# Batch transform moved into the first block of each batch, its half sums to the front of VectorE's tiles, two-product values in second blocks

## The chip, the cores and the metric

The kernel runs on one core of a Trainium2 chip. The metric is the device time of one execution in microseconds, median of three runs. The core's engines work in parallel, each through its own stream of instructions in order: TensorE (PE; its weight loads are listed as PEld), VectorE (DVE), ScalarE (ACT), GpSimd (POOL) and SyncE (SP, which here only issues DMAs). Matmul results land in PSUM, eight banks of 128 x 512 float32; GpSimd cannot read them.

## What is computed

```python
def _attn_ref(x):                       # x: (8, 3008, 256)
    X = np.fft.fft(x, axis=1)
    X = np.fft.fft(X, axis=2)
    return X.real.astype(np.float32)

def _moe_ref(x, w_gate, w_val, w_out):  # x: (24064, 256), 256 -> 1536 -> 256
    gate = np.maximum(x @ w_gate, 0.0)
    val = x @ w_val
    return (gate * val @ w_out).astype(np.float32)
```

The real part of a two-dimensional Fourier transform of each of 8 batches goes into a gated feed-forward layer.

## The kernel before, in words

**Mathematics.** The transform along the sequence is folded by symmetry into a cosine part U and a sine part V, 128 channels by 1505 columns each, one column per pair of rows s and S - s. The transform along the channels is folded into the weights: WA (cosine) and WB (sine), index 0 for the gate and 1 for the value; WM is -2 times WB except in its row 0. So for one chunk f of 128 of the 1536 hidden features, WA·U + WB·V is the hidden row of the "plus" half and WA·U - WB·V that of the "minus" half. What belongs to channel 128 is kept in one row per batch, spread over the partitions in a tile CB, and added by a per-partition scale b2.

**Tiles.** In batch 0 the columns go in four segments. From batch 1 on they go in three blocks, `thirds`: 512, 512 and 481 columns. A block has 12 tiles, one for each chunk `fi`. A tile makes both halves of the hidden h for its columns. The call `slot(cur, mid, nxt, after, outs, fold_us)` (L1072) writes the instructions of one tile's time: it finishes `pending` (the tile before), makes the value of `cur`, and prepares the gates of the two after. The order in which a slot issues work is the order on each engine. The parts, by line:

- `sine_part` (L1018): a product into bank g (L1021), copied to SBUF by ScalarE (L1024). `seed` (L1011): ScalarE puts the channel-128 part into a bank p (L1016). `cosine_part` (L1026): one product added to it (L1028).
- `both` (L1030): VectorE makes the gate of the plus half (L1032), GpSimd that of the minus half (L1033).
- `value` (L924): two products into a bank v (L876, L877); VectorE's `relu_mult` (L912) multiplies gate and value into h. One tile later `mirror` adds a third product (L882) so that v holds the minus half's value, and a second `relu_mult` reads it. That is five products of 512 columns for a plain tile: L1021, L1028, L876, L877, L882.
- A **two-product value** (`st["short"]`) uses bank d, of which there is one: ScalarE seeds it (`seed_value`, L1049), one product makes the cosine part (`value_cosine`, L1053), ScalarE copies twice that to SBUF (L1054), a second product completes the plus half (`value_sine`, L1058). The minus half is the difference, taken by VectorE in `value_second`: back into d where `own` is set (L1065), with VectorE's multiplication behind it, or into SBUF (L1067), with GpSimd's multiplication behind it (L1068) and a Relu of the gate on ScalarE (L1129). Such a tile has four products.
- A **"j" tile** makes its gate without g and without `both`: ScalarE copies twice the cosine part out of p (L1039), a second product completes it (L1043), ScalarE copies that (L1044), GpSimd subtracts (L1045). Its products are five.

In batches 2 to 5 the third block (`blk == 2`) is "mixed": tiles 2 and 8 have two-product values with `own`, tiles 5 and 11 are j tiles. The third block of batch 6 and the first two of batch 7 have two-product values in tiles 2, 6 and 10 (`SHORT`), the last block of batch 7 in 2, 5 and 8.

**Output products.** The h of a finished block are multiplied by `wo` during the next block: `todo_out` holds these steps (L784, 256 columns each), 96 for a block or 84 where the last block of a batch leaves one unit less. A slot issues `outs` of them, five eighths between its sine and its cosine product and the rest at its end. ScalarE copies a finished pair out (L797, the queue `evict`, one per slot), and SP sends it to memory.

**The transform of the next batch.** `dft_steps` makes 24 products, eight groups of three (L589), all into bank d: for each of two families, V and then U, a group for one parity, which ScalarE copies to `es` (L598), then a group added to it for the other, which ScalarE casts to the result (L601) and from which VectorE makes the other result in two half sums (L603). `DFT_EVEN[at]` says how many steps are issued behind slot `at` (0 to 35) of a batch: three behind 0, 2, 6, 8, 12, 14, 18 and 20. The copies go to the front of `evict`, the half sums to `sums`, and a slot runs one of each at its end. Two DMAs of the next batch's CB and of row 0 of its V ride on step 21.

**The folds.** GpSimd folds the rows of the batch after next (`fold_steps`): each step has a cost in units, 20.8 in all, and each slot gives `fold_us` of credit, .72, until they are used up. Among the steps SP is told to load the mirrored rows of the batch after that (`load_reversed`, L189, into XG) and to write the reversed copy of a later one (`reverse`, L180, to xr). The first readers of XG are the next batch's `fold_a` (L198).

Of the kernel before, what the change touches and what calls it, by code (L numbers as in the profile page):

```python
# [34 lines left out]
def kernel(  # L35
# [8 lines left out]
    nc = tc.nc  # L44
    B, S, D = x.shape
# [411 lines left out]
    for t in range(3):  # L457
        n = ROWS[1][t]
# [98 lines left out]
            return dst[:, 0:NJ], dst[:, NJ:2 * NJ]  # L557
        return dst[:, 3 * NJ:4 * NJ + 1], dst[:, 2 * NJ:3 * NJ]

    evict, sums = [], []  # L560

    def flush():
        for todo in (evict, sums):
            while todo:
                todo.pop(0)()

# [3 lines left out]
    def family(b, dst, fam, sine, now=True, pool=None):  # L570

        n, cols = (NE, slice(0, NE)) if fam == 0 else (NJ, slice(NE, NK))
        src, tab = (GG[b % 2], tabS) if sine else (FF[b % 2], tabC)
        st, apart = {}, now or pool is not None

        def mm(par, t, nyq=False):
            if par not in st and not apart and not par:
                st[0] = st[1]  # L580
            elif par not in st:
                home, tag = pool or ((psG, "g") if now and not par else (psD, "d"))
                st[par] = home.tile([128, 512], F32, name=tag, tag=tag)
            rows = slice(0, ROWS[par][t])
            if nyq:
                nc.tensor.matmul(st[par][0:1, 0:n], lhsT=FF[b % 2][rows, fam, t, par, 128:129], rhs=tabC[rows, 2 * t + par, cols],
                                 start=False, stop=(t == 2), skip_group_check=True)
            else:
                nc.tensor.matmul(st[par][:, 0:n], lhsT=src[rows, 1 - fam if sine else fam, t, par, 0:128],  # L589
                                 rhs=tab[rows, 2 * t + par, cols], start=(t == 0 and (apart or par == 1)), stop=(t == 2),  # L590
                                 skip_group_check=not apart)
                if b > 2 and (fam, sine, par, t) == (0, False, 0, 2):
                    widen(st[par], n)

        def end(par):
            if par:
                st["es"] = rp.tile([128, NE], F32, name="es", tag="es", bufs=2)
                evict.insert(0, lambda: nc.scalar.copy(st["es"][:, 0:n], st[1][:, 0:n]))  # L598
            elif not apart:
                whole, rest_ = half_of(dst, fam)  # L600
                evict.insert(0, lambda: nc.scalar.copy(whole, st[1][:, 0:n]))  # L601
                for c in (slice(0, NJ // 2), slice(NJ // 2, NJ)):
                    sums.append(lambda c=c: nc.vector.scalar_tensor_tensor(rest_[:, c], in0=st["es"][:, c], scalar=2.0, in1=st[1][:, c],  # L603
                                                                           op0=ALU.mult, op1=ALU.subtract))
            else:
                for d, op in zip(half_of(dst, fam), (ALU.add, ALU.subtract)):
                    m = d.shape[-1]
                    sums.append(lambda d=d, op=op, m=m: nc.vector.tensor_tensor(d, st["es"][:, 0:m], st[0][:, 0:m], op=op))
            if now:
                flush()  # L610

        def at(par):
            home, tag = pool
            st[par] = home.tile([128, 512], F32, name=tag, tag=tag)
            return st[par]
        return mm, end, at

    def dft_first(U, V):

        raw, ends = [], [family(0, dst, 1, False, now=False, pool=pool) for dst, pool in ((U, (psP, "p")), (V, (psO, "o")))]  # L620
        bank = {(k, par): ends[k][2](par) for k in range(2) for par in (1, 0)}

        def products(t, k, rs):
            src, tab = ((FF[1], tabC), (GG[1], tabS))[k]
            for r, par in [(r, par) for r in rs for par in (1, 0)]:
                rows = slice(0, ROWS[par][t])
                nc.tensor.matmul(bank[k, par][:, 0:NJ], lhsT=src[rows, r, t, par, 0:128], rhs=tab[rows, 2 * t + par, odd_k],
                                 start=(t == 0 and r == 0), stop=(t == 2 and r == 1), skip_group_check=bool(k))

        def nyquist(t):  # L630
            for par in (1, 0):
                rows = slice(0, ROWS[par][t])
                nc.tensor.matmul(bank[1, par][0:1, 0:NJ], lhsT=ny[rows, t, par:par + 1], rhs=tabC[rows, 2 * t + par, odd_k],
                                 start=False, stop=False, skip_group_check=True)

        def combine(i, js):
            for j in js:
                home, tag = ((psV, "v"), (psV, "v"), (psG, "g"), (psD, "d"))[len(raw)]
                p = home.tile([128, 512], F32, name=tag, tag=tag)
                for kc in range(2):  # L640
                    nc.tensor.matmul(p[:], lhsT=(TA, TB)[j][:, kc, :], rhs=wr[i][0][:, kc, :], start=(kc == 0), stop=(kc == 1))
                raw.append(p)

        def whole(W, p):
            return W[:, 0:512], p[:]

        products(0, 0, (0,))
        products(0, 1, (0,))
        whole_128(0)
        angle(4, 5)  # L650
        products(0, 0, (1,))
        products(0, 1, (1,))
        nyquist(0)
        angle(5, 4)
        whole_128(1)
        for T in (TA, TB):
            nc.scalar.copy(T[:, 1, 0::2], T[:, 0, 0::2])
            nc.scalar.mul(T[:, 1, 1::2], T[:, 0, 1::2], -1.0)
        products(1, 0, (0, 1))
        products(1, 1, (0, 1))  # L660
        nyquist(1)
        combine(0, (0, 1))
        nc.scalar.copy(*whole(WA[0], raw[0]))
        whole_128(2)
        products(2, 0, (0, 1))
        ends[0][1](1)
        ends[0][1](0)
        evict.pop(0)()
        nc.vector.tensor_scalar(m2[:], pidx[:], scalar1=1.0, op0=ALU.min, scalar2=-2.0, op1=ALU.mult)
        sums[0]()  # L670
        nc.scalar.copy(*whole(WB[0], raw[1]))
        nyquist(2)
        products(2, 1, (0, 1))
        ends[1][1](1)
        ends[1][1](0)
        evict.pop(0)()
        sums[2]()
        combine(1, (0, 1))
        nc.scalar.copy(*whole(WA[1], raw[2]))
        nc.scalar.copy(*whole(WB[1], raw[3]))  # L680
        for k in (1, 3):
            sums[k]()
        del sums[:]
# [160 lines left out]

    DFT_0 = (0, 0, 0, 0, 0, 3, 0, 0, 4, 3, 3, 0), (0, 0, 0, 0, 0) + (1,) * 7, (3, 3, 3, 3, 3, 3, 0, 0, 0, 0, 0, 0)

    DFT_EVEN = (3, 0, 3, 0, 0, 0) * 4 + (0,) * 12
    DFT_1 = (3, 0, 3, 0, 0, 0) * 4 + (0, 1, 0, 1, 1) + (0,) * 7
    todo_out, todo_dft, todo_fold = [], [], []
    credit, paired = 0, False  # L850
    pending = None
# [7 lines left out]
    def run_one(todo):  # L859
        if todo:  # L860
            todo.pop(0)()
# [134 lines left out]
    SHORT = (2, 6, 10)  # L996

    def new_tiles():
        for b in range(1, B):
            for blk, block in enumerate(thirds):  # L1000
                for fi in range(NF):
                    st = tile_of(block, fi, uv[b])
                    st["b"] = b
                    mixed = 1 < b < 6 and blk == 2
                    st["kind"] = "o" if (b, blk, fi) == (1, 0, 6) else "j" if mixed and fi in (5, 11) else "n"
                    st["own"] = mixed
                    st["short"] = mixed and fi in (2, 8) or (b, blk) in ((6, 2), (7, 0), (7, 1)) and fi in SHORT or (b, blk) == (7, 2) and fi in (2, 5, 8)
                    st["lead"] = (b, blk, fi) == (1, 0, 0)
                    yield st

# [61 lines left out]
    def slot(cur, mid, nxt, after, outs, fold_us):  # L1072

        joined, ready = (st is not None and st["kind"] == "j" for st in (nxt, mid))
# [5 lines left out]
            run(todo_out, len(todo_out) - stop + outs * part // 8)  # L1080
        old = nxt is not None and nxt["kind"] == "o"
        new = nxt is not None and nxt["kind"] == "n"
        if old:
            gate(nxt)
        lead = cur["lead"]
# [44 lines left out]
        if nxt is not None and nxt["short"]:  # L1130
            seed_value(nxt)
        run_fold(fold_us)
        if not joined:
            run_one(evict)
        run_one(sums)
        out(8)
        return cur

# [1 line left out]
    tiles, ahead = new_tiles(), []  # L1140

    for b in range(B):
# [4 lines left out]
        for blk, block in enumerate(blocks):  # L1147
            hs = []
            if (b, blk) == (0, 1):
                todo_dft = dft_steps(0, U, V, (0,), nyq=True, now=True)  # L1150
# [69 lines left out]
            else:  # L1220
                for fi in range(NF):
                    at = NF * blk + fi
                    cur = ahead.pop(0)
                    add_h(cur, hs)
                    ahead.append(next(tiles, None))
                    outs = per_tile + ((-2, 0, -2, 2, 2, 0)[fi % 6] if per_tile == 7 else 0)
                    if (b, blk) == (B - 1, 2) and fi > 8:
                        outs = (10, 9, 19)[fi - 9]
                        if fi == 9:
# [5 lines left out]
                        nc.scalar.mul(WV[:, f], WM[1][:, f], -0.5)  # L1235
                    if (b, at) == (2, 0):
                        nc.sync.dma_start(out=WB[0][0:1, :], in_=WM[0][0:1, :])
                    pending = slot(cur, *ahead, outs, .72)
                    for step in more_1.get(at, ()) if b == 1 else ():
                        step()  # L1240
                    run(todo_dft, DFT_1[at] if b == 1 else DFT_EVEN[at])
# [44 lines left out]
```

## Time and profile before

| | |
|---|---|
| median of three runs | 625.36 us (625.28 to 625.39) |
| the profiled execution | 625.38 us |
| its span | 623.5 us |
| instructions | 12412 |
| granted TensorE clock, mean | 1.000 |
| busy VectorE / ScalarE / GpSimd | 547.9 / 473.6 / 516.4 us |

The profile is of one execution. Starts and lengths of instructions are recorded; the ends of matmuls are modelled, so neighbouring matmuls overlap in the record and the time of one is read from start to start. VectorE's and ScalarE's records overlap a little too where one instruction follows on another. A few matmul records can be missing. "Busy" of a window is the time in which the engine has at least one instruction.

### The profile page before, as it was taken

How to read it: one execution, taken by the hardware profiler on the slowest of the kernel's cores; microseconds unless marked ns; L12 is line 12 of the kernel's file. 1: busy time of each engine (PE TensorE's matmuls, PEld its weight loads, DVE VectorE, ACT ScalarE, POOL GpSimd, SP SyncE). 2: the span in 40 equal slices, each digit the busy share in tenths (PEclk: the TensorE clock that was granted, in tenths of full speed). 3: DMA queues.
4: the chain of work that ended last, by engine and by line, in shares of the span. 5: the costliest groups of instructions: out<-in, count | busy, mean ns of one | idle time of the engine just before them, and what ended most of it. 6: DMA issues, size and time to landing. Idle time of an engine off the chain costs nothing.

```text
span 623.5 us, 12412 instructions
## 1 busy us (share of the span) xinstructions
PE 614.8 (99%) x4043; PEld 396.4 (64%) x4087; DVE 547.9 (88%) x978; ACT 473.6 (76%) x878; POOL 516.4 (83%) x490
## 2 busy tenths in 40 slices
PE   8999999999999999999999999999999999999997
PEld 2566666566666666666666666666666666666666
DVE  8886677999899899988999999999999999999991
ACT  7796667777778778776887778777787768999982
POOL 8988992998899988799879989799886656888881
PEclk9999999999999999999999999999999999999999
DMA  9965658744264427315362425211211111211113
GB/s 241 213 200 135 169 181 92 183 88 144 85 152 143 131 71 178 122 45 167 79 189 69 142 77 120 64 54 49 77 44 55 43 61 37 61 52 53 44 51 104
DMA packets 86034, 66.48 MB, mean 107 GB/s; under 512 B 41639, under 2 KB 69063, under 8 KB 85970
## 3 DMA queue, kind: packets, MB, share of 16 engines
q1 hardware_dynamic: 81384, 60.02, 35.4%
q0 software_dynamic: 3984, 4.92, 4.0%
q8 instruction: 32, 0.52, 0.4%
q10 hardware_dynamic: 602, 0.75, 0.4%
q14 instruction: 32, 0.26, 0.1%
HBM read 41.89 MB, written 34.17 MB: 122 GB/s over the span
## 4 chain that ended last, share of the span: by engine, by line
PE 95%; DVE 1%; POOL 1%; issue 1%; DMA 1%; ACT 0%; DVEq 0%; POOLq 0%; ACTq 0%
PE o L784 38%; PE v L882 10%; PE v L877 10%; PE p L1028 8%; PE g L1021 8%; PE v L876 8%; PE d L589 4%; PE p L882 1%; PE p L876 1%; PE p L877 1%; DMA XG<-in_x_dram,gidx 1%; PE d L1053 1%; PE d L1058 1%; PE o L427 1%; POOL XG L120 1%
## 5 line engine op out<-in xcount | busy, mean ns | idle before, releaser
L1033 POOL TENSOR_TENSOR r<-r 128x512 f32<-128x512 f32 (+1 forms) x243 | 302.7, 1253 | 80.2 <-DVE r L1032 77.3
L784 PE MATMUL o<-wo,h 128*128 128x256 bf16 x2172 | 329.6, 273 | 0.2
L912 DVE SCALAR_TENSOR_TENSOR h<-r,v 128x512 bf16<-128x512 f32 (+1 forms) x462 | 294.3, 675 | 38.2 <-PE v L882 32.3
L784 PEld LDWEIGHTS <-h 128*128 128x128 bf16 x2220 | 216.6, 98 | 110.6 <-issue 0.9
L1016 ACT ACTIVATE p<-CB,b 128x512 f32<-128x512 bf16 (+1 forms) x251 | 172.1, 686 | 51.5 <-DVE r L1032 49.6
L1024 ACT COPY r<-g 128x512 f32<-128x512 f32 (+1 forms) x243 | 140.4, 578 | 48.3 <-PE g L1021 41.5
L1032 DVE SCALAR_TENSOR_TENSOR r<-r,p 128x512 f32<-128x512 f32 (+1 forms) x243 | 163.1, 671 | 0.8 <-ACT r L1024 0.8
L877 PE MATMUL v<-V,WB 128*128 128x512 bf16 (+3 forms) x273 | 100.1, 367 | 2.1
L1028 PE MATMUL p<-U,WA 128*128 128x512 bf16 (+1 forms) x251 | 94.1, 375 | 0.0
L1021 PE MATMUL g<-V,WM 128*128 128x512 bf16 (+1 forms) x243 | 91.2, 375 | 0.2
L882 PE MATMUL v<-V,WM 128*128 128x512 bf16 (+1 forms) x232 | 87.0, 375 | 0.2 <-DVE h L912 0.2
L876 PE MATMUL v<-U,WA 128*128 128x512 bf16 (+3 forms) x237 | 86.4, 365 | 0.0
L901 DVE TENSOR_TENSOR h<-r,v 128x376 bf16<-128x376 f32 (+2 forms) x90 | 46.2, 547 | 16.4 <-PE v L882 10.5
L876 PEld LDWEIGHTS <-WA 128*128 128x128 bf16 x328 | 31.9, 97 | 36.1 <-issue 13.4
L797 ACT COPY os<-o 128x512 f32<-128x512 f32 x92 | 52.5, 570 | 2.9 <-issue 2.9
L198 POOL TENSOR_TENSOR XG<-XG,XD 128x510 f32<-128x510 f32 x42 | 52.9, 1268 | 0.8 <-DMA XG<-xr 0.8
L892 ACT ACTIVATE r<-p 128x376 f32<-128x376 f32 (+1 forms) x80 | 38.3, 487 | 18.0 <-PE p L882 8.6
L877 PEld LDWEIGHTS <-WB 128*128 128x128 bf16 x328 | 31.9, 97 | 31.4 <-ACT WB L680 0.2
L206 POOL TENSOR_TENSOR AA<-XG 128x510 f32<-128x510 f32 x42 | 45.3, 1092 | 0.0
L1021 PEld LDWEIGHTS <-WM 128*128 128x128 bf16 x243 | 23.8, 98 | 5.6 <-issue 0.3
L1028 PEld LDWEIGHTS <-WA 128*128 128x128 bf16 x251 | 24.5, 98 | 3.3 <-issue 0.2
L882 PEld LDWEIGHTS <-WM 128*128 128x128 bf16 x233 | 22.8, 98 | 3.6
(201 smaller groups left out, 534.8 us busy)
## 6 DMA issues: line engine op xcount, KB each, us to landing
out_dram<-os SPq DMA_DIRECT2D x124, 128.0 KB
xr<-in_x_dram SPq DMA_DIRECT2D x12, 768.0 KB
XG<-xr SPq DMA_DIRECT2D x12, 768.0 KB
XD<-in_x_dram SPq DMA_DIRECT2D x15, 512.0 KB
out_dram<-os SPq DMA_DIRECT2D x35, 112.0 KB
XD<-in_x_dram SPq DMA_DIRECT2D x8, 448.0 KB
CB<-ch SPq DMA_DIRECT2D x7, 376.2 KB
out_dram<-os SPq DMA_DIRECT2D x13, 96.0 KB
```

Of the source, the lines that this page charges most:

```text
L198: e.tensor_tensor(XG[p, r, t, ::-1, 1:D], XG[p, r, t, ::-1, 1:D], XD[p, r, t, :, D - 1:0:-1], op=ALU.add)
L784: nc.tensor.matmul(st["p"][0:m, q, :], lhsT=lhs(f), rhs=wo[:, f, :], start=(f == 0 and not (early and q)), stop=(f == NF - 1), skip_group_ ...
L876: nc.tensor.matmul(bank[:, 0:st["n"]], lhsT=WA[i][:, st["f"]], rhs=st["us"], start=True, stop=False)
L877: nc.tensor.matmul(bank[:, 0:st["n"]], lhsT=WB[i][:, st["f"]], rhs=st["vs"], start=False, stop=True)
L882: nc.tensor.matmul(bank[:, 0:st["n"]], lhsT=W[i][:, st["f"]], rhs=v, start=False, stop=True, skip_group_check=True)
L912: nc.vector.scalar_tensor_tensor(half_h(st, sign), in0=st["s"][1 + sign][:, 0:n], scalar=0.0, in1=st["v"][:, 0:n], op0=ALU.max, op1=ALU.mult)
L1016: nc.scalar.activation(st["p"][:, 0:st["n"]], st["c"], ACTF.Copy, scale=b2[:, st["fi"]:st["fi"] + 1])
L1021: nc.tensor.matmul(st["g"][:, 0:n], lhsT=WM[0][:, st["f"]], rhs=st["vs"], start=True, stop=True)
L1024: nc.scalar.copy(q[:, 0:n], st["g"][:, 0:n])
L1028: nc.tensor.matmul(st["p"][:, 0:n], lhsT=WA[0][:, st["f"]], rhs=st["us"], start=False, stop=True, skip_group_check=True)
L1032: nc.vector.scalar_tensor_tensor(sp[:, 0:n], in0=q[:, 0:n], scalar=-0.5, in1=st["p"][:, 0:n], op0=ALU.mult, op1=ALU.add)
L1033: nc.gpsimd.tensor_tensor(sm[:, 0:n], sp[:, 0:n], q[:, 0:n], op=ALU.add)
```

## The change

The kernel keeps every operation's form; it changes where they stand and which tiles use which form.

- `DFT_EVEN` becomes three steps behind slots 0, 1, 3, 4, 6, 7, 9 and 10, so that the eight groups stand in the first block of batches 2 to 6. (Batch 1 has a table of its own and stays.)
- The transform's ScalarE copies get a queue of their own, `turned_out`. From batch 2 on a slot starts with one step of it and one half sum (two when no transform step is left); before batch 2 both stay at the end of the slot.
- The second block of batches 2 to 5 becomes mixed like the third, and the second block of batch 6 gets two-product values in tiles 2, 6 and 10.
- From batch 2 on the output products are issued in the pattern -1, -1, +2 around the mean in first blocks (except batch 7's) and evenly elsewhere.
- The credit of the folds becomes .76 a slot in first blocks and .54 in the others, from batch 2 on.

```diff
-    evict, sums = [], []
+    evict, sums, turned_out = [], [], []
...
-        for todo in (evict, sums):
+        for todo in (turned_out, evict, sums):
...
-                evict.insert(0, lambda: nc.scalar.copy(st["es"][:, 0:n], st[1][:, 0:n]))
+                turned_out.append(lambda: nc.scalar.copy(st["es"][:, 0:n], st[1][:, 0:n]))
...
-                evict.insert(0, lambda: nc.scalar.copy(whole, st[1][:, 0:n]))
+                turned_out.append(lambda: nc.scalar.copy(whole, st[1][:, 0:n]))
...
-    DFT_EVEN = (3, 0, 3, 0, 0, 0) * 4 + (0,) * 12
+    DFT_EVEN = (3, 3, 0) * 4 + (0,) * 24
...
-                    mixed = 1 < b < 6 and blk == 2
+                    mixed = 1 < b < 6 and blk > 0
...
-                    st["short"] = mixed and fi in (2, 8) or (b, blk) in ((6, 2), (7, 0), (7, 1)) and fi in SHORT or (b, blk) == (7, 2) and fi in (2, 5, 8)
+                    st["short"] = mixed and fi in (2, 8) or (b, blk) in ((6, 1), (6, 2), (7, 0), (7, 1)) and fi in SHORT or (b, blk) == (7, 2) and fi in (2, 5, 8)
...
         new = nxt is not None and nxt["kind"] == "n"
+        early = cur["b"] > 1
+        if early:
+            run_one(turned_out)
+            run_one(sums)
+            if not todo_dft:
+                run_one(sums)
...
-        if not joined:
+        if turned_out and not early:
+            run_one(turned_out)
+        elif not joined:
             run_one(evict)
-        run_one(sums)
+        if not early:
+            run_one(sums)
...
-                    outs = per_tile + ((-2, 0, -2, 2, 2, 0)[fi % 6] if per_tile == 7 else 0)
+                    if b < 2:
+                        outs = per_tile + ((-2, 0, -2, 2, 2, 0)[fi % 6] if per_tile == 7 else 0)
+                    else:
+                        outs = per_tile + (0 if blk or b == B - 1 else (-1, -1, 2)[fi % 3])
...
-                    pending = slot(cur, *ahead, outs, .72)
+                    pending = slot(cur, *ahead, outs, .72 if b < 2 else (.76, .54, .54)[blk])
```

More of the change, by code (lines that the diff above doesn't have):

```diff
@@ L667, in dft_first @@
         ends[0][1](0)
-        evict.pop(0)()
+        turned_out.pop(0)()
         nc.vector.tensor_scalar(m2[:], pidx[:], scalar1=1.0, op0=ALU.min, scalar2=-2.0, op1=ALU.mult)
@@ L675, in dft_first @@
         ends[1][1](0)
-        evict.pop(0)()
+        turned_out.pop(0)()
         sums[2]()
```

## The prediction

> **What bounds the kernel now.** I read the page first (share of each engine), then the tensor engine's own timeline inside one tile, then the busy time by stretches of one block, and last the waits. The page:
>
> ```profile
> PE 614.8 (99%) x4043; PEld 396.4 (64%) x4087; DVE 547.9 (88%) x978; ACT 473.6 (76%) x878; POOL 516.4 (83%) x490
> ```
>
> The ends of matmuls are modelled, so the 99% proves little alone. The timeline of TensorE through one tile of batch 2 (start, length, what) settles it:
>
> ```profile
> 206.05 0.71 PE L784 MATMUL o<-wo,h 128*128 128x256 bf16 x5
> 206.60 0.38 PE L1028 MATMUL p<-U,WA 128*128 128x512 bf16 x1
> 206.81 0.38 PE L882 MATMUL v<-V,WM 128*128 128x512 bf16 x1
> 207.03 0.38 PE L876 MATMUL v<-U,WA 128*128 128x512 bf16 x1
> 207.25 0.38 PE L877 MATMUL v<-V,WB 128*128 128x512 bf16 x1
> 207.46 0.49 PE L784 MATMUL o<-wo,h 128*128 128x256 bf16 x3
> 207.79 0.65 PE L589 MATMUL d<-tabS,G 128*128 128x377 bf16 x3
> 208.27 0.38 PE L1021 MATMUL g<-V,WM 128*128 128x512 bf16 x1
> 208.49 0.71 PE L784 MATMUL o<-wo,h 128*128 128x256 bf16 x5
> ```
>
> Starts, not lengths, give the price. From 206.60 to 207.46 four products of 512 columns start 0.215 us apart; five output products take 206.60 - 206.05 = 0.55, so 0.109 each; three transform products take 208.27 - 207.79 = 0.48, so 0.160 each. Nothing stands between them: TensorE streams, and a plain 512-column tile lasts 8 x 0.109 + 5 x 0.215 = 1.95 us. So this kernel's time in these batches is a count of matmuls, until another engine falls behind. Busy time by block (a row is one block of 12 tiles; length, then each engine's busy time and instructions):
>
> ```profile
> 177.53:202.21 24.68, 24.49 (x158) 15.42 (x158) 23.09 (x41) 19.82 (x35) 23.84 (x21) 1.00 0.60 166
> 202.21:227.67 25.46, 25.30 (x169) 16.48 (x170) 23.05 (x41) 18.49 (x34) 23.77 (x25) 1.00 0.38 112
> 301.25:323.67 22.42, 22.42 (x155) 14.86 (x153) 21.27 (x37) 18.63 (x35) 19.72 (x16) 1.00 0.59 148
> 469.80:494.48 24.68, 24.49 (x157) 15.42 (x158) 23.09 (x41) 19.11 (x33) 15.54 (x13) 1.00 0.16 48
> 494.48:519.94 25.46, 25.30 (x168) 16.47 (x169) 23.05 (x41) 18.07 (x33) 15.14 (x13) 1.00 0.17 52
> 542.44:565.45 23.01, 22.86 (x153) 14.93 (x154) 22.03 (x37) 21.01 (x38) 18.69 (x16) 1.00 0.16 48
> 565.45:588.43 22.98, 22.82 (x153) 14.96 (x153) 22.11 (x37) 20.88 (x38) 18.73 (x16) 1.00 0.15 47
> ```
>
> Rows one and two are blocks 0 and 1 of batch 2, row three is block 2 of batch 3, four and five are blocks 0 and 1 of batch 6, six and seven those of batch 7. Batch 7 is the row to learn from: its blocks have no transform and three two-product tiles each, at 512 columns, which is nearly what the change makes of block 1 in batches 2 to 6. The granted clock is 1.00 in every row.
>
> **The change part by part.**
>
> *The transform moves.* Its 24 products (eight groups of three) in each of batches 2 to 6 stood in tiles 0 to 20, four groups in each of blocks 0 and 1; now all stand in block 0. Block 0 gains 12 x 0.160 = 1.92 us, block 1 loses as much: **sum 0**. With it move eight ScalarE copies and eight half sums. The DMA pair of the row of channel 128 and the row 0 of V, which rides on step 21, goes out at tile 10 instead of 20; its readers are in the next batch, so SP is the only one to feel it, and earlier. The output products are dealt out 7, 7, 10 (or 6, 6, 9) in block 0 so that tiles with a transform group are not the longest; their number is the same, price 0.
>
> *Two-product values are added.* Block 1 of batches 2 to 5 gets two such tiles (and two "j" tiles) each, block 1 of batch 6 three: 4 x 2 + 3 = 11 tiles, each with one 512-column product fewer. **11 x 0.215 = -2.37 us** on TensorE.
>
> The Trainium skill, page "TensorE: Matmul & The Clock Gate", section "Back-to-back issue gap", says that a stream of weight loads and 512-column matmuls sustains about 131 ns each, and that 216 ns is the gap of an isolated one. By it the eleven would be worth an estimated 11 x 0.131 = 1.44 us. The trace here disagrees: 0.215 in the full stream above.
>
> *What they cost the other engines.* These forms are in the trace, in batch 7 (instructions by line and shape: busy us, mean ns):
>
> ```profile
> L1049 ACT ACTIVATE d<-CB,b 128x512 f32<-128x512 bf16 x6 | 4.0, 673 | 0.0
> L1054 ACT ACTIVATE r<-d 128x512 f32<-128x512 f32 x6 | 3.5, 582 | 0.0
> L1067 DVE TENSOR_TENSOR r<-r,d 128x512 f32<-128x512 f32 x6 | 4.1, 682 | 0.0
> L1033 POOL TENSOR_TENSOR r<-r 128x512 f32<-128x512 f32 x167 | 211.8, 1273 | 62.8 <-DVE r L1032 60.1 <-DMA out_dram<-os 2.2
> L603 DVE SCALAR_TENSOR_TENSOR V<-es,d 128x188 bf16<-128x188 f32 x24 | 8.2, 344 | 0.0
> ```
>
> A two-product tile adds 0.67 + 0.58 us on ScalarE and one 0.68 us subtraction on VectorE. A j tile takes a 0.68 us `both` off VectorE and puts a copy of about 0.58 on ScalarE. In batches 2 to 5 that is for block 1: VectorE 2 - 2 = 0 instructions, less the four half sums that leave; ScalarE about 2 x 1.25 + 2 x 0.58 = 3.7 us more, less the four transform copies, near the 21.01 us of batch 7's block, inside 23 us. In batch 6 the three subtractions on VectorE are paid back by three minus products that go to GpSimd, which has no folds there (15.14 us of 25.46). So both are covered by the tensor engine, VectorE with little room (22.03 busy of 23.01 in batch 7). If that cover were gone, each 0.68 us operation that VectorE is late would come straight onto the time.
>
> What remains visible is small. Next to a two-product tile fewer output products are issued, so the mirror product of the tile before comes early and waits for VectorE, which is still reading that bank. First row VectorE, then TensorE:
>
> ```profile
> 550.78 1.29 DVE L912 SCALAR_TENSOR_TENSOR h<-r,v 128x512 bf16<-128x512 f32 x2
> ...
> 551.81 0.38 PE L1028 MATMUL p<-U,WA 128*128 128x512 bf16 x1
> 552.12 0.38 PE L882 MATMUL v<-V,WM 128*128 128x512 bf16 x1
> ```
>
> The pair on VectorE ends at 552.07, the mirror starts at 552.12, 0.31 after the product before it instead of 0.215: a wait of 0.09 us. The block rows give the same size in another way: batch 6's block 1 should lose 12 x 0.160 + 3 x 0.215 = 2.57 us to become like batch 7's, but 25.46 - 23.00 = 2.46; about 0.1 us per block stays behind. I take 0.09 per block from the first, **5 x 0.09 = +0.45 us**; bounds: 0 (the waits that block 1 has today go too) and one wait per two-product tile, 11 x 0.09 = 1.0.
>
> *Front of the tile.* The half sums and the ScalarE copy move from the end of one tile's stream to the start of the next. On VectorE's stream the end of tile k and the start of tile k + 1 are neighbours, so no work is added; but only one tile, no longer two, lies between a bank's last reader and the next group into it. VectorE around two sums today:
>
> ```profile
> 208.50 0.68 DVE L1032 SCALAR_TENSOR_TENSOR r<-r,p 128x512 f32<-128x512 f32 x1
> 209.74 1.28 DVE L912 SCALAR_TENSOR_TENSOR h<-r,v 128x512 bf16<-128x512 f32 x2 [0.55 <-PE v L882]
> 210.94 0.68 DVE L1032 SCALAR_TENSOR_TENSOR r<-r,p 128x512 f32<-128x512 f32 x1
> 211.54 0.34 DVE L603 SCALAR_TENSOR_TENSOR V<-es,d 128x188 bf16<-128x188 f32 x1
> 211.80 1.28 DVE L912 SCALAR_TENSOR_TENSOR h<-r,v 128x512 bf16<-128x512 f32 x2
> ```
>
> The tile whose sine product starts at 208.27 has its first VectorE work at 209.74 (1.47 later) and its last starts at 210.94, and would make room for the next at 211.54, 3.27 after the tile began. In the new order the first half sum falls into the idle 0.55 us ahead of 209.74; the second stands at 3.27 and takes 0.26 to the next start (0.34 to its end). The next group into the bank starts at the end of the tile after: 2.17 us (a tile of 10 output products) + 7 x 0.109 + 5 x 0.215 = 4.0. Margin 4.0 - 3.6 = 0.4 us, or 0.3 since one more output product stands ahead of the mirror; with 9 and 6 products 2.06 + 1.73 = 3.8, margin 0.2. Price taken: 0. Bounds: a gain of 0.1 us a batch at most, since those sums now lie in idle time, and a loss worked out as a rival below.
>
> *GpSimd's folds.* Their rate goes from .72 a tile to .76, .54, .54. The work is the same; by the code's own counts (20.8 units a batch) they end at tile 33 of 36 instead of 28, and block 1's GpSimd load falls from 23.77 us of 25.46 by 12 x .18 = 2.2, while block 0 takes .5 more in a block that is 1.9 longer. Late next is the load of the following batch's mirrored rows, issued with the last folds: tile 30 instead of 26, or 4 x 22.42 / 12 = 7.5 us. Today (SP's timeline, GpSimd's, then GpSimd's busy time with the DMA share and GB/s at the end of the row):
>
> ```profile
> 307.16 1.36 SPq L189 DMA_DIRECT2D XG<-xr  x2
> ...
> 329.81 1.27 POOL L198 TENSOR_TENSOR XG<-XG,XD 128x510 f32<-128x510 f32 x1
> ...
> 310.00:313.00 3.00, 3.00 (x3) 1.00 1.06 227
> 313.00:316.00 3.00, 3.00 (x4) 1.00 1.06 205
> 316.00:319.00 3.00, 2.19 (x3) 1.00 0.55 155
> ```
>
> Issue at 307.16, DMA saturated until about 316, first use at 329.81. So 8.9 us of transfer in 22.6; after the change 15.1 remain, margin about 6. Price 0; if the cover were gone GpSimd would stand at the fold with the tiles' own subtractions queued behind it.
>
> **The sum:** 0 - 2.37 + 0.45 = -1.92 us on the profiled execution's 625.38 us (span 623.5 and 1.9 around it; the runs' median is 625.36, so the two are the same for this purpose). **Forecast 623.4 us.** Its own bounds: 2.37 + 0.1 x 5 off gives 622.5, 2.37 - 1.0 off gives 624.0.
>
> **The rivals.**
>
> 1. *VectorE becomes the pace of block 1 (no change).* For it: 22.03 us busy of 23.01 in batch 7's block. Against: its instructions start every 0.60 us (210.94 to 211.54), 36 x 0.60 = 21.6 against 23.2 us of block. If each of the 11 new tiles upset both its neighbours, 22 x 0.09 = 2.0 us would come back: 625.38 - 2.37 + 2.0 = 625.0.
>
> 2. *The single transform bank is handed over too late (slower).* One mechanism, at the start of a new group in block 0: three such starts behind a second half sum and four behind a ScalarE copy per batch, 35 in all. For it: margin of 0.2 us with 9 and 6 products, and half the spacing of before. Against: VectorE has 5.4 + 0.52 us of work in three tiles of 6.5 to 6.8. It eats the gain when each start waits 1.92 / 35 = 0.055 us, and the kernel is slower beyond that; at 0.15 us each, 35 x 0.15 - 1.92 = +3.3: 628.7.
>
> 3. *The mirrored rows land late.* It decides beyond the 6 us of margin, and then with about 2 us in three batches (the loads for folds in batches 3 to 5): 625.38 - 1.92 + 6 = 629.5. Against it stands this row, the only wait for that load in the span:
>
> ```profile
> POOL XG L198 <- DMA XG<-xr: 0.8, 1, 0.8
> ```
>
> 4. *A 512-column product gives back less than its start-to-start time*, for instance only the 0.109 of an output product: -11 x 0.109 + 0.45 = -0.75, 624.6. The block rows speak against it (2.46 of 2.57 came).
>
>    By the Trainium skill's rule above (page "TensorE: Matmul & The Clock Gate", section "Back-to-back issue gap") it would be an estimated 625.38 - 1.44 + 0.45 = 624.4; the 0.215 of this trace disagrees.
>
> **How the numbers follow.** Forecast .72, rival 1 .14, rival 2 .07, rival 3 .03, rival 4 .04. About 0.2% (1.25 us) is what a measurement of this kernel can tell from no change: faster means below 624.1, slower above 626.6. Faster .72; same .18 (rivals 1 and 4); slower .10 (2 and 3). The range 622.7 to 625.0 holds most of the forecast's case, half of rival 1 and rival 4, some 8 in 10; the forecast's own is 622.5 to 624.0.
>
> **What would show it.** Block 1 of batch 2 should last about 23.2 us (batch 7's 23.0 and one product more) without a half sum in it; block 0 about 26.6; batch 6's blocks 26.6 and 23.0. Products by the mirror line fall by 11. Transform groups should start with no gap to the output product ahead of them, else rival 2; the waits list should show no larger wait of GpSimd's fold on its load, else rival 3; mirror products that start over 0.1 us late in every tile of block 1 mean rival 1. The forecast is wrong if block 0 grows by clearly more than 1.92 us or block 1 shrinks by less than 2.1.

## The result, and the profile after

The changed kernel takes **622.01 us** (median of six runs, 621.70 to 622.17) against 625.36 us (six runs, 625.28 to 625.47): a ratio of 0.9946, 95% interval 0.9933 to 0.9959. That is 3.35 us faster, outside the measurement's noise, and 1.4 us below the forecast of 623.4; it lies below the range, too. The profiled execution is the fastest of the six, 621.70 us with a span of 619.6.

The page after, first the engines:

```profile
PE 610.7 (99%) x4032; PEld 395.3 (64%) x4076; DVE 549.5 (89%) x978; ACT 485.4 (78%) x911; POOL 520.5 (84%) x493
```

TensorE has eleven instructions fewer, VectorE as many as before, ScalarE 33 more. The blocks after, in the same windows as in the prediction (blocks 0 and 1 of batch 2, block 2 of batch 3, blocks 0 and 1 of batch 6):

```profile
177.35:203.67 26.32, 26.16 (x171) 16.66 (x172) 24.60 (x46) 20.88 (x39) 25.45 (x23) 1.00 0.58 160
203.67:226.80 23.13, 22.97 (x154) 15.06 (x155) 22.12 (x37) 19.75 (x36) 21.57 (x21) 1.00 0.35 117
299.79:322.11 22.32, 22.32 (x155) 14.85 (x153) 21.09 (x37) 18.58 (x35) 20.07 (x16) 1.00 0.44 100
466.86:493.17 26.31, 26.15 (x171) 16.66 (x172) 24.59 (x46) 19.72 (x37) 15.95 (x13) 1.00 0.16 49
493.17:516.15 22.98, 22.82 (x153) 14.95 (x154) 21.94 (x36) 20.89 (x38) 17.39 (x14) 1.00 0.18 54
```

Block 1 came as forecast (23.13 for 23.2 and 22.98 for 23.0). Block 0 of batch 2 did not: it grew by 26.32 - 24.68 = 1.64 us instead of 1.92, although its twelve transform products cost what they should. Batches 4 and 6 are like it; in batches 3 and 5, where the first block has 96 output products, it grew by 2.04 (25.42 to 27.46): there the window holds one output product more, and only 0.075 us of waits were there to lose. Even the third block, whose tiles keep their forms, is 0.10 us shorter in batch 3 (22.32 for 22.42). So something else went besides the products.

Whole times of one kernel scatter by about a microsecond from chip to chip and run to run. What follows is therefore read from one stretch, from the cosine product of batch 2's first tile to that of batch 7's first tile, in which everything lies that was edited. Its length is the number right behind the window's two ends; before, then after:

```profile
177.53:542.44 364.91, 363.24 (x2392) 236.09 (x2420) 337.37 (x582) 281.20 (x497) 309.43 (x265) 1.00 0.34 94
```

```profile
177.35:538.55 361.20, 359.62 (x2381) 235.24 (x2409) 339.00 (x582) 293.06 (x530) 313.90 (x268) 1.00 0.34 95
```

The stretch lost 3.71 us. A second profile of the changed kernel, on another chip (`e10_after_again`), gives 361.21, and the two profiles of the filled kernel below give 359.43 and 359.41, so differences of a few hundredths can be read here. What the forecast did not hold is seen at a mirror product of the kernel before, behind the half sums of batch 2 (VectorE, then TensorE):

```profile
213.59 0.34 DVE L603 SCALAR_TENSOR_TENSOR V<-es,d 128x188 bf16<-128x188 f32 x1
213.85 1.28 DVE L912 SCALAR_TENSOR_TENSOR h<-r,v 128x512 bf16<-128x512 f32 x2
...
214.89 0.38 PE L1028 MATMUL p<-U,WA 128*128 128x512 bf16 x1
215.18 0.38 PE L882 MATMUL v<-V,WM 128*128 128x512 bf16 x1
```

The mirror stands 0.29 us behind the product ahead of it, where 0.215 is the price of that product: VectorE's pair ended at 213.85 + 1.28 = 215.13. A wait of 0.075 us; there were such in every batch. Read in this way over the whole stretch, mirrors waited 3.63 us in 42 places before and 2.23 us in 26 places after.

No transform group waits after the change, although the margin is as small as the prediction had it. Changed kernel, VectorE's second half sum and the next group into the bank, in batch 2:

```profile
191.05 0.34 DVE L603 SCALAR_TENSOR_TENSOR U<-es,d 128x188 bf16<-128x188 f32 x1
...
191.25 0.49 PE L784 MATMUL o<-wo,h 128*128 128x256 bf16 x3
191.58 0.65 PE L589 MATMUL d<-tabS,G 128*128 128x377 bf16 x3
```

The half sum ends at 191.39, the group starts at 191.58, right behind three output products of 0.109: margin 0.19 us, no stall.

### The profile page after: what moved, and what is told of

Its sections match the earlier page's. It is cut to its first block, busy times and chain, and to the rows that moved or that the text cites. A ratio compares the mean times of both kernels' runs of the same rounds, so it can differ in the third digit from the quotient of the medians.

```text
span 619.6 us, 12415 instructions
## 1 busy us (share of the span) xinstructions
PE 610.7 (99%) x4032; PEld 395.3 (64%) x4076; DVE 549.5 (89%) x978; ACT 485.4 (78%) x911; POOL 520.5 (84%) x493
## 4 chain that ended last, share of the span: by engine, by line
PE 95%; DVE 1%; POOL 1%; issue 1%; DMA 1%; ACT 0%; DVEq 0%; POOLq 0%; ACTq 0%
PE o L784 39%; PE v L877 10%; PE v L882 9%; PE p L1028 8%; PE g L1021 8%; PE v L876 7%; PE d L589 4%; PE p L882 1%; PE d L1058 1%; PE d L1053 1%; PE p L876 1%; PE p L877 1%; DMA XG<-in_x_dram,gidx 1%; PE o L427 1%; PE p L1043 1%
## 5 line engine op out<-in xcount | busy, mean ns | idle before, releaser
L1033 POOL TENSOR_TENSOR r<-r 128x512 f32<-128x512 f32 (+1 forms) x235 | 293.4, 1254 | 75.0 <-DVE r L1032 73.8
L912 DVE SCALAR_TENSOR_TENSOR h<-r,v 128x512 bf16<-128x512 f32 (+1 forms) x440 | 281.0, 674 | 32.9 <-PE v L882 24.6
L1024 ACT COPY r<-g 128x512 f32<-128x512 f32 (+1 forms) x235 | 135.9, 578 | 30.8 <-PE g L1021 27.6
L1032 DVE SCALAR_TENSOR_TENSOR r<-r,p 128x512 f32<-128x512 f32 (+1 forms) x235 | 157.4, 670 | 0.8 <-ACT r L1024 0.8
L877 PE MATMUL v<-V,WB 128*128 128x512 bf16 (+3 forms) x265 | 97.0, 366 | 2.2
L1021 PE MATMUL g<-V,WM 128*128 128x512 bf16 (+1 forms) x235 | 88.2, 375 | 0.2
L882 PE MATMUL v<-V,WM 128*128 128x512 bf16 (+1 forms) x221 | 82.8, 375 | 0.2 <-DVE h L912 0.2
L876 PE MATMUL v<-U,WA 128*128 128x512 bf16 (+3 forms) x223 | 81.1, 364 | 0.0
L912 DVE SCALAR_TENSOR_TENSOR h<-r,d 128x512 bf16<-128x512 f32 (+1 forms) x47 | 31.3, 667 | 0.0
L1021 PEld LDWEIGHTS <-WM 128*128 128x128 bf16 x235 | 23.0, 98 | 5.5 <-issue 0.3
```

The source lines that it names most:

```text
L876: nc.tensor.matmul(bank[:, 0:st["n"]], lhsT=WA[i][:, st["f"]], rhs=st["us"], start=True, stop=False)
L877: nc.tensor.matmul(bank[:, 0:st["n"]], lhsT=WB[i][:, st["f"]], rhs=st["vs"], start=False, stop=True)
L882: nc.tensor.matmul(bank[:, 0:st["n"]], lhsT=W[i][:, st["f"]], rhs=v, start=False, stop=True, skip_group_check=True)
L912: nc.vector.scalar_tensor_tensor(half_h(st, sign), in0=st["s"][1 + sign][:, 0:n], scalar=0.0, in1=st["v"][:, 0:n], op0=ALU.max, op1=ALU.mult)
L1021: nc.tensor.matmul(st["g"][:, 0:n], lhsT=WM[0][:, st["f"]], rhs=st["vs"], start=True, stop=True)
L1024: nc.scalar.copy(q[:, 0:n], st["g"][:, 0:n])
```

## The experiments

All were compared with the kernel before on the same chip, whose medians there were 625.63 to 625.69 us. "Stretch" is the window above. The theory going in: a two-product value is worth its product less a wait at a mirror, and the rest of the gain is mirror waits of before that went with the move.

### The move alone

The changed kernel without its new two-product values:

```diff
-                    mixed = 1 < b < 6 and blk > 0
+                    mixed = 1 < b < 6 and blk == 2
...
-                    st["short"] = mixed and fi in (2, 8) or (b, blk) in ((6, 1), (6, 2), (7, 0), (7, 1)) and fi in SHORT or (b, blk) == (7, 2) and fi in (2, 5, 8)
+                    st["short"] = mixed and fi in (2, 8) or (b, blk) in ((6, 2), (7, 0), (7, 1)) and fi in SHORT or (b, blk) == (7, 2) and fi in (2, 5, 8)
```

> The changed kernel without its eleven new two-product values (second blocks plain again); the transform is packed, with the new front of the tile, output pattern and fold rates. Theory 1 (a new two-product tile is worth its one product, 0.215 us, less a wait of 0.09 at a mirror; the rest of the gain is mirror waits of before that went with the move): 625.36 - 2.0 to - 2.3, so 623.1 to 623.5. Rival (the move is worth nothing, as the prediction had it, and a two-product tile is worth 3.35 / 11 = 0.30 us): 625.1 to 625.5.

Measured 623.45 us, ratio 0.9966 (0.9954 to 0.9978). Its stretch:

```profile
177.38:540.23 362.85, 362.77 (x2423) 236.28 (x2421) 340.74 (x582) 278.89 (x497) 310.27 (x265) 1.00 0.33 94
```

364.91 - 362.85 = 2.06 us come from a move that leaves the number of products as it was. The rival falls; the two-product values bring 362.85 - 361.20 = 1.65.

### The front of the tile without the packing

The move alone, but with the old places of the groups and the old pattern of output products; what is left of the change is the front of the tile and the fold rates.

```diff
-    DFT_EVEN = (3, 3, 0) * 4 + (0,) * 24
+    DFT_EVEN = (3, 0, 3, 0, 0, 0) * 4 + (0,) * 12
...
-                    if b < 2:
+                    if True:
                         outs = per_tile + ((-2, 0, -2, 2, 2, 0)[fi % 6] if per_tile == 7 else 0)
```

> The kernel before with only the front of the tile and the new fold rates: transform groups behind tiles 0, 2, 6, 8 and so on, old pattern of output products, no new two-product values. Theory 1 (the mirror waits of before went because packed groups make every tile of block 0 longer than VectorE's work in it, and leave block 1 without half sums): the waits stay, 625.0 to 625.6. Rival (they went because half sums at the front lie in VectorE's idle time): as the move alone, 623.2 to 623.7.

Measured 624.18 us, ratio 0.9978 (0.9969 to 0.9987): between the two. Its stretch, then VectorE around the same half sums and TensorE at the mirror behind them:

```profile
177.83:541.20 363.37, 361.78 (x2393) 236.20 (x2420) 340.15 (x582) 280.37 (x497) 309.77 (x265) 1.00 0.34 94
```

```profile
209.30 0.34 DVE L603 SCALAR_TENSOR_TENSOR V<-es,d 128x188 bf16<-128x188 f32 x1
209.93 1.28 DVE L912 SCALAR_TENSOR_TENSOR h<-r,v 128x512 bf16<-128x512 f32 x2 [0.29 <-PE v L882]
211.14 0.68 DVE L1032 SCALAR_TENSOR_TENSOR r<-r,p 128x512 f32<-128x512 f32 x1
211.73 0.34 DVE L603 SCALAR_TENSOR_TENSOR V<-es,d 128x188 bf16<-128x188 f32 x1
...
215.09 0.38 PE L1028 MATMUL p<-U,WA 128*128 128x512 bf16 x1
215.30 0.38 PE L882 MATMUL v<-V,WM 128*128 128x512 bf16 x1
```

The first half sum now fills time in which VectorE waited for TensorE anyway (0.55 us before, 0.29 left), so VectorE comes out of the two sums earlier by one of them, and the mirror starts 0.21 behind its neighbour: no wait. In the second blocks no mirror waits any more, and the first mirror wait of the third blocks, 0.097 us behind the last half sum, is gone too. The run moved ScalarE's copies to the front as well; that the half sums count rests on what the mirrors waited for, VectorE. The front gives 364.91 - 363.37 = 1.54 us, 0.31 a batch. Packing and the new pattern give the other 363.37 - 362.85 = 0.52. My theory had the larger part on the wrong one of the two.

### The pattern of the output products

On the kernel before, batches 2, 4 and 6 get seven products in each tile of the first block:

```diff
-                    outs = per_tile + ((-2, 0, -2, 2, 2, 0)[fi % 6] if per_tile == 7 else 0)
+                    outs = per_tile + ((-2, 0, -2, 2, 2, 0)[fi % 6] if per_tile == 7 and b < 2 else 0)
```

> The kernel before with one edit: where a first block has 84 output products (batches 2, 4 and 6), they are dealt out 7 a tile instead of 5, 7, 5, 9, 9, 7. Theory 1 (tiles with five put only three products ahead of the mirror, which then waits 0.09 to 0.19 us for VectorE): 0.37 us in each of three batches goes, 625.36 - 1.1 = 624.3. Rival (the waits come from the place of the half sums, not from the pattern): 625.2 to 625.5.

Measured 626.45 us, ratio 1.0013 (1.0004 to 1.0022): slower, a miss for both. The stretch and one mirror behind a half sum:

```profile
177.87:543.47 365.60, 365.28 (x2422) 236.06 (x2420) 337.38 (x582) 279.62 (x497) 309.62 (x264) 1.00 0.34 94
```

```profile
186.86 0.34 DVE L603 SCALAR_TENSOR_TENSOR V<-es,d 128x188 bf16<-128x188 f32 x1
187.12 1.28 DVE L912 SCALAR_TENSOR_TENSOR h<-r,v 128x512 bf16<-128x512 f32 x2
...
188.04 0.38 PE L1028 MATMUL p<-U,WA 128*128 128x512 bf16 x1
188.45 0.38 PE L882 MATMUL v<-V,WM 128*128 128x512 bf16 x1
```

The wait is 0.41 - 0.215 = 0.19 us though four products stand ahead of the mirror. The old pattern had put nine products where the half sums are; with seven (7 x 0.109 + 5 x 0.215 = 1.84 us) such a tile is shorter than VectorE's work in it (3 x 0.60 + 0.26 = 2.06). So "fewer than four ahead" is not the whole of it: what counts here is the tile's length against VectorE's work in that tile.

The other way round, the changed kernel with the old pattern (the `if True` above, alone):

> The changed kernel with the pattern of output products of before (5, 7, 5, 9, 9, 7 where there are 84, eight everywhere else). Theory 1: waits come back in the tiles with five products, 0.2 to 0.37 us in each of three batches: 622.0 + 0.6 to 1.1 = 622.6 to 623.1. Rival (pattern without effect): 621.9 to 622.2.

Measured 622.62 us, ratio 0.9954 (0.9940 to 0.9968). Its stretch:

```profile
177.54:539.11 361.57, 361.57 (x2412) 235.15 (x2410) 339.19 (x582) 293.01 (x530) 313.70 (x268) 1.00 0.34 95
```

0.37 us longer than the changed kernel's. The time lies at the lower end of what was expected, but the waits of 0.2 us did not come back: in batches 2, 4 and 6 one wait of 0.09 us did. The pattern is worth some 0.4 us in all.

### Filling the wait

On the changed kernel, the tile ahead of a two-product tile puts four of its six output products, not three, ahead of its cosine product, and so ahead of the mirror:

```diff
-        out(4 if lead or nxt is None else 5)
+        out(4 if lead or nxt is None else 6 if mid["short"] and cur["b"] > 1 else 5)
```

> The changed kernel, but from batch 2 on the tile ahead of a two-product tile, which has six output products, puts four instead of three of them ahead of its cosine product. Theory 1 (the mirror there waits 0.08 to 0.11 us for VectorE, while output products stand behind it that could run): of some 30 such waits most go, 622.0 - 2.0 to - 2.7 = 619.3 to 620.0. Rival (VectorE sets the pace there, so the wait comes at the next mirror): 621.8 to 622.2.

Measured **619.78 us**, ratio 0.9909 (0.9894 to 0.9924); again on another chip, as `e12_filled_again`, 620.01, ratio 0.9908 (0.9894 to 0.9922). It beats both kernels. First the changed kernel at a mirror ahead of a two-product tile in batch 2, then the filled one at the same tile:

```profile
205.40 0.38 PE L1028 MATMUL p<-U,WA 128*128 128x512 bf16 x1
205.71 0.38 PE L882 MATMUL v<-V,WM 128*128 128x512 bf16 x1
```

```profile
205.92 0.38 PE L1028 MATMUL p<-U,WA 128*128 128x512 bf16 x1
206.13 0.38 PE L882 MATMUL v<-V,WM 128*128 128x512 bf16 x1
```

0.31 us became 0.21. Nothing but the order of TensorE's own products was changed, so VectorE is not the pace of these blocks.

On the kernel before, the same idea for tiles with five or six products:

```diff
-        out(4 if lead or nxt is None else 5)
+        out(4 if lead or nxt is None else {5: 7, 6: 6}.get(outs, 5) if cur["b"] > 1 else 5)
```

> The kernel before; from batch 2 on tiles with five or six output products put four instead of three of them ahead of the cosine product. Theory 1 (a mirror wait ends with VectorE's reading of bank v, and output products behind it could run meanwhile): the waits in tiles with five or six go, 0.37 x 3 in batches 2, 4 and 6, 0.2 in each third block of batches 2 to 6 and 0.2 in each of two blocks of batch 7: 625.5 - 2.0 to - 2.6 = 622.9 to 623.5. Rival (the lag of VectorE only moves to the next tile, as with the even pattern): 625.2 to 626.4.

Measured 623.18 us, ratio 0.9960 (0.9946 to 0.9973), as expected; its stretch is 2.13 us shorter than before, and batch 7 lies outside it:

```profile
177.93:540.71 362.78, 361.21 (x2391) 236.15 (x2419) 337.65 (x582) 281.67 (x497) 309.28 (x264) 1.00 0.34 94
```

### What a two-product value is worth without the wait

The move alone with the fill, beside the filled kernel:

> The move alone (second blocks plain, as in e1_move_only) with the fill of e4_fill_wait. Theory (with the mirror waits filled, a two-product value is worth exactly its product): 619.8 + 11 x 0.215 = 622.1. Rival (new two-product values bring or save something besides): outside 621.8 to 622.5.

> The kernel of e4_fill_wait again, beside the others on this chip: 619.5 to 620.1 by every theory.

> The changed kernel again, beside the others on this chip: 621.8 to 622.3 by every theory.

Measured 621.69, 620.01 and 622.24 us, ratios 0.9938 (0.9924 to 0.9953), 0.9908 and 0.9946 (0.9932 to 0.9960). The first missed its theory and, by its letter, fell to the rival: it lies 0.1 us beyond the lower end of 621.8 to 622.5. The stretch decides. The stretches, of the move alone and of the filled kernel:

```profile
177.53:539.34 361.81, 360.16 (x2392) 236.34 (x2420) 340.96 (x582) 279.10 (x497) 310.31 (x265) 1.00 0.34 95
```

```profile
178.36:537.77 359.41, 357.82 (x2382) 235.34 (x2409) 339.53 (x582) 293.10 (x530) 313.69 (x268) 1.00 0.34 95
```

361.81 - 359.41 = 2.40 us for eleven products, 0.218 each: close to the start-to-start time of the trace, 0.215, that the prediction took. About 0.1 of the 2.40 is a mirror wait in batch 2 that got shorter (0.24 to 0.13 us). The whole times differ by 1.68 only. The other 0.7 lies ahead of and behind the stretch, where the two kernels are the same; two profiles of the changed kernel differ there by as much (span less stretch: 619.6 - 361.20 = 258.4 and 620.3 - 361.21 = 259.1).

### The hand-over of bank d at the end of the tile

The changed kernel, with the transform's copies and half sums at the end of a tile:

```diff
-        early = cur["b"] > 1
+        early = False
...
-        if not early:
+        for _ in range(1 if todo_dft or cur["b"] < 2 else 2):
             run_one(sums)
```

> The changed kernel with the transform packed, but its ScalarE copies and half sums at the end of a tile as before (both half sums of the last group in the tile behind it). Theory (packing is possible only because the hand-over of bank d is at the front): the second half sum ends some 3.6 us after its tile began and the next group would start at 1.84, a stall of up to 1.8 us at 3 places in each of 5 batches; a ScalarE copy ends at about 2.6, a stall of about 0.7 at 4 places: 622 + 20 to 40 = 642 to 662. Rival (the end of one tile and the front of the next are neighbours in VectorE's stream, so it makes no difference): 622.0 to 622.5.

Measured 671.71 us, ratio 1.0735 (1.0719 to 1.0752). A second half sum, the next group and the stretch:

```profile
187.37 0.34 DVE L603 SCALAR_TENSOR_TENSOR V<-es,d 128x188 bf16<-128x188 f32 x1
...
187.77 0.66 PE L589 MATMUL d<-tabC,F 128*128 128x376 bf16 x3 [1.76 <-DVE V L603]
```

```profile
177.76:592.64 414.88, 374.54 (x2401) 238.21 (x2434) 343.36 (x588) 298.69 (x537) 317.92 (x271) 0.99 0.30 83
```

The stall at a half sum is about what was worked out (1.76 us idle for "up to 1.8"; 1.8 to 2.0 at such places when read from start to start). The 35 group starts of the stretch came late by 35.3 us in all, inside the 20 to 40 expected: fifteen behind a second half sum make most of it, and twenty behind a ScalarE copy cost only 0.26 to 0.37 each, not 0.7. But the stretch grew by 53.7 us. Three output products that start 2.97 us late add 8.9; the rest was not taken apart. So the mechanism of rival 2 is real and dear; at the front of the tile it just does not decide.

### The fold rates

The changed kernel with .72 in every tile:

> The changed kernel with the fold rate of before, .72 in every tile. Theory (the rates cost and bring nothing): 621.8 to 622.4. Rival (in the shorter second block, 23.1 us, GpSimd with 12 x (1.23 + .72) = 23.4 us of work sets the pace): some 0.3 to 1 us in each of four batches, 623.2 to 626.

Measured 622.21 us, ratio 0.9945 (0.9932 to 0.9959); stretch 361.21 against 361.20:

```profile
177.61:538.82 361.21, 359.65 (x2382) 235.17 (x2410) 339.13 (x582) 292.92 (x530) 313.03 (x268) 1.00 0.34 95
```

The rates are worth nothing either way.

### A third two-product value

The filled kernel with one more such value in the mixed blocks:

```diff
-                    st["short"] = mixed and fi in (2, 8) or (b, blk) in ((6, 1), (6, 2), (7, 0), (7, 1)) and fi in SHORT or (b, blk) == (7, 2) and fi in (2, 5, 8)
+                    st["short"] = mixed and fi in (2, 6, 9) or (b, blk) in ((6, 1), (6, 2), (7, 0), (7, 1)) and fi in SHORT or (b, blk) == (7, 2) and fi in (2, 5, 8)
```

> e4_fill_wait with a third two-product value in the mixed blocks of batches 2 to 5 (tiles 2, 6 and 9 instead of 2 and 8): eight products fewer, eight VectorE subtractions more, 37 instead of 36 a block. Theory (TensorE still sets the time, 37 x 0.60 = 22.2 us of VectorE in 22.7 us): 619.8 - 8 x 0.215 = 618.1, less some 0.1 a block in waits, 618.1 to 618.9. Rival (VectorE is now the pace of these blocks): 619.6 to 621.

Measured 624.98 us, ratio 0.9990 (0.9981 to 0.9999): 5 us lost, a miss for both. Waits in a window over batch 3's second and third block (us in total, times, longest):

```profile
ACT d L1049 <- DVE h L912: 2.1, 2, 1.1
...
PE d L1053 <- ACT d L1049: 1.0, 2, 0.5
```

Tiles 6 and 9 share bank d three tiles apart. The seed of the second waits about 1 us for VectorE to read the first, and the product behind the seed waits for it. Read from start to start, these eight products come 0.62 to 0.68 us late each, 5.2 us in all, about what was lost. So the bank decided; whether VectorE's 37 instructions alone would fit was not tried with other tiles.

## Why the prediction was wrong, point by point

- **The eleven products, -2.37 us: right.** With the waits filled they are worth 2.3 to 2.4, so rival 4 falls. By the Trainium skill (page "TensorE: Matmul & The Clock Gate", section "Back-to-back issue gap") it would have been an estimated 1.44; the runs disagree.
- **The waits that the new tiles bring, +0.45 us: too small as their price, near as a net.** I read them from the difference between batch 6's block 1 and batch 7's. That difference of 0.1 us is a net one: waits behind half sums had gone from it while others had come. In the second blocks after the change there is a wait ahead of each of the eleven tiles, 11 x 0.09 = 1.0, the bound that I had put at the other end. Against the move alone the net is some 0.75, since one wait in batch 2 fell from 0.24 to 0.03 us. The fill takes 0.78 us off the second blocks (0.17 or 0.18 in batches 3 to 5, 0.26 in batch 6; in batch 2 nothing, where waits come back at a later tile). Set against the kernel before, mirror waits in the five second blocks grew from 0.65 to 1.01 us, a net 0.36 and so near the 0.45; that block 1 came out as forecast is in part the luck of this, new waits in the place of old ones.
- **"*Front of the tile* ... Price taken: 0": this is the step that failed.** The text saw that the first half sum would fall into VectorE's idle time, and bounded its gain by 0.1 us a batch. The runs show 1.54 us, 0.31 a batch, which alone is more than the 1.4 us by which the forecast missed. What I missed is what VectorE's lag was costing: its waits stood in the trace of before, in all three blocks, and I priced the ones to come without listing those that were there. Mirror waits in the five first blocks fell from 1.44 to 0.17 us and in the third blocks from 1.54 to 1.04; the forecast had nothing for either. The direction, that sums in idle time gain something, was right; the size was not.
- **The move, "sum 0", and the output pattern, "price 0": off by 0.52 us together.** The products cost the same wherever they stand, but how much longer a tile is than VectorE's work in it depends on them. With the old pattern the changed kernel's stretch is 0.37 us longer, so by that run the pattern is the larger part; the packing by itself was not run.
- **The folds and the mirrored rows, price 0: right.** The rates do nothing, and the wait for the load is 0.9 us for 0.8. Changed kernel, the list of waits:

```profile
POOL XG L198 <- DMA XG<-xr: 0.9, 1, 0.9
```

- **The rivals.** Rival 1 (VectorE the pace) falls with the fill. Rival 2's margin of 0.2 us was measured as 0.19, and its price as 1.8 to 2.0 us behind a half sum once the margin is gone. Rival 3 did not happen.

In the stretch: front 1.54, packing and pattern 0.52, two-product values 1.65 (2.40 less 0.75 in waits); together the 3.71 us. The forecast had 0, 0 and 1.92.

That the waits at the mirror are the cause can be checked over nine of the kernels. In each, the waits are summed by starts, as in the section on the result (0.216 us taken as the price of a 512-column product and 0.203 of a 481-column one; waits under 0.02 left out):

| kernel | stretch, us | mirror waits, us (places) | stretch less waits |
|---|---|---|---|
| before | 364.91 | 3.63 (42) | 361.28 |
| before, even pattern | 365.60 | 4.43 (42) | 361.17 |
| before, four ahead | 362.78 | 1.55 (22) | 361.23 |
| front not packed | 363.37 | 2.03 (23) | 361.34 |
| move alone | 362.85 | 1.48 (15) | 361.37 |
| move alone, filled | 361.81 | 0.41 (4) | 361.40 |
| changed | 361.20 | 2.23 (26) | 358.97 |
| changed, old pattern | 361.57 | 2.54 (30) | 359.03 |
| changed, filled | 359.41 | 0.30 (4) | 359.11 |

What is left in the last column is the same to 0.23 us in the six kernels without the new two-product values and to 0.14 us in the three that have them, some 2.3 us lower.

## What to carry to other kernels

Where one engine streams, list its small waits by place before pricing an edit: here output products put ahead at thirty-one places gained 2.2 us, nearly what the eleven products gave. A net difference between two blocks is no price for a wait, since old waits may have left it. In this kernel, work that can start early belonged ahead of the instruction that waits, where it filled idle time; and when a product waits for another engine, putting independent products of the same engine ahead of it was worth trying.

## What the runs showed of the hardware that was not expected

In these traces VectorE's recorded lengths are longer than its pace: a 512-column operation is listed with 0.68 us, and the next starts 0.60 us after it (210.94 to 211.54 in the prediction's rows). By the listed lengths three of them would be 2.04 us, longer than the plain tile's 1.95, and VectorE would be the bound; by the starts they are 1.80.
